# Splitting the last 64 rows of a weight matrix once, apart from the rest

## The chip, the cores and the metric

The kernel runs on one NeuronCore of one Trainium2 chip. The metric is the device time in microseconds (us) of one execution, as the median of several runs. The profile comes from one more execution. TensorE (PE) does the matrix products, VectorE (DVE), ScalarE (ACT) and GpSimd (POOL) the elementwise work, and all transfers are issued from the queue of SyncE (SP).

## The reference

A sequence of 2048 tokens with 576 features goes through a layernorm, linear attention with 32 heads and, beside it, a feed-forward network (FFN) with 4608 hidden features; the FFN's output gates the attention's. Everything is float32.

```python
xn = _layernorm(x)                       # x: [1, 2048, 576]
# attention: q, k, v = xn @ wqkv in 32 heads of 18 features
phi = lambda t: jnp.where(t > 0, t + 1, jnp.exp(t)) + 1e-6
kv = jnp.einsum("bhsd,bhse->bhde", phi(k), v);  z = phi(k) summed over s
s = ((phi(q) @ kv) / (phi(q) @ z + 1e-6)) @ wo
# FFN: w1 [576, 4608], w2 [4608, 576]
g = silu(gelu(xn @ w1 + b1) @ w2 + b2)
out = x + s * g
```

## The kernel before

**Number format.** PE multiplies in a reduced format, fp32r. To keep float32 accuracy each operand is split into a high part (an ACT copy to fp32r, "hi") and a low part (the rest, by a DVE subtraction, "lo"), and a product is the sum of three matmuls: hi x hi, hi x lo and lo x hi.

**Phase 1 (0 to about 155 us)** loops over 16 tiles of 128 tokens, `t` = 0 to 15, one per 9.05 us. In each turn PE projects keys and values (`project`, L222), transposes a later tile (`transpose_x`, L199) and adds up the attention's state (`state`, L259). `layernorm(t + 2)` runs on DVE, POOL (`mv`, L176) and ACT (`xn`, L194). Since nothing else needs it yet, the loop also makes differences of blocks of `w2` for the FFN: `w2_sum` (POOL, L291), `w2_hi` (ACT, L299), `w2_lo` (DVE, L304), `w2_store` (L309), with raw loads `w2_load` (L277). `zacc` (POOL, L425) sums the keys.

**Phase 2 (to about 291 us)** makes queries and the attention's output `s`.

**Phase 3, the FFN**, works on halves of 1024 tokens with 9 chunks of 512 hidden features each: 18 steps. Both matrix products of a step use a 2x2 block scheme with 7 products in place of 8 (Strassen's, in Winograd's form), whose operands are sums and differences of blocks. The up-projection of a step handles two *pairs* of `w1`, `n = 2 * step` and `n + 1`; `Up.step` takes the seven products in the order `UP = (1, 6, 7, 5, 2, 3, 4)`, each seven matmuls of 128x512 (L901): three for each of two blocks of 128 rows, and one for the last rows. Those, 64 of `w1`'s 576 and so 32 in each half of the block scheme, are put together as three copies of 32 rows on the partitions of one tile (`r`), two hi and one lo, so that one matmul makes all three products. Results are combined on DVE: `b` (L927), `e` (L934), `zy` (L938), `mid` (L921, L924), with an ACT copy `mid` (L918) and the GELU on ACT (`g`, L909). Then come 14 groups of 12 down matmuls (`product`, L1031), each added into the accumulator `macc` by DVE (L1040).

**The operands of w1.** In the first half, class `W1` loads a pair raw (`w1raw`, 768 KB, L621; the last rows already copied three times by the host, hence `WT = 6` blocks), makes the differences `T` on POOL (L636 to L645), the hi parts on ACT (L649) and the lo parts on DVE: L657 for the whole blocks and L659 for the 32 partitions of the last rows' lo part. The finished tiles are kept in DRAM (`keep_op`, L600). In the second half class `W1Loaded` (L682) loads them back. Tiles `a`, `c` and `d` (10 blocks of 128 columns) hold two operands each, from a ring of four buffers; tile `6` holds one, from two buffers.

**The operands of w2.** `W2.hi` (L603) and `W2.lo` (L606) split the pieces of `w2` that phase 1 has not made. L603 and L606 also split the hidden activations `h`.

**The bias b2.** `start_with_b2` (L867) fills `macc` with copies of `b2` by two broadcast transfers, at step 0 and again at step 9.

**Order.** A step has 28 slots: `base + 7j + k` behind product `k` of pair `j`, then `base + 14 + 2k + q` behind the down groups. `add(slot, fn)` puts work into a slot, and DVE, ACT, POOL and PE execute in exactly that order; the SP queue's order is the scheduler's. Tables place the work: `P1` for the odd pair during its own step, `P0` for the next step's even pair, `PW2` for `w2`.

Of the kernel before, what the change touches and what calls it, by code (L numbers as in the profile page):

```python
# [15 lines left out]
P = 128  # L16
# [8 lines left out]
KT = 5  # L25
WT = 6
NF = F // P
# [12 lines left out]
@with_exitstack  # L40
def linear_attention_gated_ffn(ctx, tc, x, wqkv, wo, w1, b1, w2, b2, out):
    nc = tc.nc
# [68 lines left out]


    rr_dram = dram.tile([2, P, 512], F32, name="rr_dram")
    rq_dram = dram.tile([2, 8, P, 512], F32, name="rq_dram")
    c_dram = dram.tile([2, P, QH, 2, HD], F32, name="c_dram")

# [194 lines left out]

    W2_LOADS = {0: (0, 1), 1: (2,), 3: (3,), 4: (4,), 5: (5,), 8: (6,), 9: (7,), 12: (8,)}
    W2_SUMS = {}
# [80 lines left out]
    for t in range(NT):  # L394
        if t + 3 < NT:
            load_x(t + 3)
        pk = bank2(f"pk{t}")
        project(t, wk_h, wk_l, pk)
        if t == 0:
            for k in range(KT):  # L400
                split_w(raw_v[k], k, wv_h, wv_l, nc.vector)
        if t + 1 < NT:
            if t + 1 in (8, 12):
                x_block((t + 1) // 4)
            transpose_x(t + 1)
        for j in W2_SUMS.get(t - 1, ()):
            w2_hi(j)
        for j in W2_SUMS.get(t - 1, ()):
            w2_lo(j)
        if t + 2 < NT:  # L410
            layernorm(t + 2)
        k_t, _ = phi(t1, pk, f"k{t}")
        if pend is not None:
            state(*pend)
        pv = bank2(f"pv{t}")
        project(t, wv_h, wv_l, pv)
        v_t = t1.tile([P, D], F32, tag="v", name=f"v{t}")
        nc.scalar.copy(as2(v_t), pv[:, :, :HD])
        if t + 2 < NT:
            normalize_x(t + 2)  # L420
        if t == 0:
            nc.gpsimd.memset(zacc, 0.0)
        for j in W2_SUMS.get(t, ()):
            w2_sum(j)
        nc.gpsimd.tensor_tensor(zacc, zacc, k_t, op=ADD)  # L425
        for k in WQ_SPLITS.get(t, ()):
            split_w(raw_q[k], k, wq_h, wq_l, nc.gpsimd if k == 0 else nc.vector)
        for k in WQ_LOADS.get(t, ()):
            raw_q[k] = load_w_raw(0, k)
        for j in W2_SUMS.get(t - 1, ()):  # L430
            w2_store(j)
        for c in W2_LOADS.get(t, ()):
            w2_load(c)
        if t == KT + 2:
            make_mask()
            nc.gpsimd.memset(kvz, 0.0)
        pend = (t, k_t, v_t)
        if t in (4, 8):
            b = t // 4 - 1
            if b == 0:  # L440
                nc.sync.dma_start(x_dram[:, 0:4], xh[0][:, :4].bitcast(F32))
                nc.sync.dma_start(x_dram[:, 4:8], xl[0].bitcast(F32))
            else:
                nc.sync.dma_start(x_dram[:, 10:12], xh[1][:, 2:4].bitcast(F32))
                nc.sync.dma_start(x_dram[:, 14:16], xl[1][:, 2:].bitcast(F32))
# [162 lines left out]


    def w1_tile(i, n):  # L610
        k, tag, bufs = (5, "w6", 2) if i == 6 else (10, "wa", 4)
        return w1p.tile([P, k, P], F32R, tag=tag, name=f"w{i}_{n}", bufs=bufs)

    class W1:


# [11 lines left out]
        def T(self, i):  # L628


            a, b = slice(0, 3), slice(3, 6)
            f0, f1, src = self.f0, self.f1, self.src
            tt = EW1.tensor_tensor
            if i == 5:
                src[5] = f0[:, a]
                tt(src[5], f1[:, a], f0[:, a], op=SUB)  # L636
            elif i == 6:
                src[6] = w1p.tile([P, 3, P], F32, tag="w1t6", name="w1t6", bufs=1)
                tt(src[6], f1[:, b], src[5], op=SUB)
            elif i == 7:  # L640
                src[7] = f1[:, a]
                tt(src[7], f1[:, b], f1[:, a], op=SUB)
            else:
                src[4] = f0[:, b]
                tt(src[4], f0[:, b], src[6], op=SUB)  # L645

        def hi(self, i):
            self.tiles[i] = t = w1_tile(i, self.n)
            nc.scalar.copy(t[:, : 3 if i == 6 else 6], self.src[i])  # L649

        def lo(self, i):
            t, src = self.tiles[i], self.src[i]
            n = 1 if i == 6 else 2
            by3 = lambda v: v.rearrange("p (h k) c -> p h k c", h=n)
            hi, src = by3(t[:, : 3 * n]), by3(src)
            lo = t[:, 3 * n :].rearrange("p (h k) c -> p h k c", h=n)
            EL1.tensor_tensor(lo, src[:, :, :2], hi[:, :, :2].bitcast(F32), op=SUB)  # L657
            r = hi[64:96, :, 2]
            EL1.tensor_tensor(r, src[64:96, :, 2], r.bitcast(F32), op=SUB)  # L659
            keep_op(w1_dram, (self.n, i), t)  # L660

        def product(self, i):

            if i == 6:
                t = self.tiles[6]
                return t[:, :2], t[:, 3:], t[:, 2]
            key, k = {1: "a0", 2: "a1", 7: "c0", 3: "c1", 5: "d0", 4: "d1"}[i]
            t, k = self.tiles[key], int(k)
            return t[:, 3 * k : 3 * k + 2], t[:, 6 + 2 * k : 8 + 2 * k], t[:, 3 * k + 2]

    class W1Loaded(W1):


        def __init__(self, n):
            self.n, self.tiles = n, {}
            for i in ("a", 6, "c", "d"):
                if i == "c":
                    t = w1r.tile([P, 10, P], F32R, tag="stw", name=f"wc_{n}")
                else:
                    t = w1_tile(i, n)  # L680
                self.tiles[i] = t
                nc.sync.dma_start(t.bitcast(F32), w1_dram[n % NP, i])  # L682
# [17 lines left out]
    class Rest:  # L700
# [30 lines left out]
        def split(self, k):  # L731
# [3 lines left out]
            nc.vector.tensor_tensor(l, src, h.bitcast(F32), op=SUB)  # L735
            for n, v in enumerate((h, l, h, h)):
                nc.sync.dma_start(
                    rq_dram[self.half, 4 * k : 4 * k + 4, 32 * n : 32 * n + 32], v.bitcast(F32)
                )
# [8 lines left out]

    def load_rest(half, i, dst):
        nc.sync.dma_start(dst.bitcast(F32), rq_dram[half, REST_AT[i]])  # L750

# [24 lines left out]
    def beside(i, k):  # L776
# [15 lines left out]
        else:  # L792
# [16 lines left out]
            if i == 13:  # L809
                w1t[1] = W1(1)  # L810
            if i == 16:
                z = xsum[1]
                load_rest(1, 1, z.h0[:, 4])
                load_rest(1, 6, z.tiles[0][:, 4])
                load_rest(1, 7, z.h1[:, 4])
            if i == 17:
# [4 lines left out]
                w.hi(6), w.lo(6)  # L821
            if i == 18:
                w = w1t[0]
                for j in ("c", "d"):
# [39 lines left out]
    C11, C12, C21, C22, U1 = range(5)  # L864
    def start_with_b2():
        for b in range(2):
            nc.sync.dma_start(  # L867
                macc[:, :, 2 * b : 2 * b + 2].rearrange("p q h d -> p q (h d)"),
                bass.AP(tensor=b2.tensor, offset=b2.offset, ap=[[0, P], [0, QH], [1, D]]),
            )  # L870

# [149 lines left out]
    def product(c, i, q2, hs, w, held):  # L1021
# [14 lines left out]
        src, dst = ps[:, :, :HD], macc[:, q2 : q2 + 2, DST[i], :]  # L1036
        if c == 0 and i == 1:
            nc.vector.tensor_copy(dst, src)
        else:
            nc.vector.tensor_tensor(dst, src, dst, op=ADD)  # L1040

# [9 lines left out]
    def load_xs(t):  # L1051
        F = lambda v: v.bitcast(F32)
        if t in (0, 3):
            raw = stage_w1(f"xs{t}")
            xt, s_t = raw[:, :D], raw[:, KT * P : KT * P + D]
        elif t < 5:
            raw = w1_tile("a", f"xs{t}") if t < 4 else fr.tile(
                [P, 2, D], F32R, tag="w2_5", name="xs4", bufs=1
            )
            raw = F(raw).rearrange("p a b -> p (a b)")  # L1060
            xt, s_t = raw[:, :D], raw[:, D : 2 * D]
        else:
# [132 lines left out]
    def plan_w1(add, w, base, T, hi, lo):  # L1195
# [5 lines left out]
        T={5: 1, 6: 1, 7: 1, 4: 2},  # L1201
        hi={"a": 0, 6: 2, "c": 4, "d": 5},
        lo={"a": 0, 6: 3, "c": 4, "d": 6},
    )
# [39 lines left out]
    xs = x_operands(z.h0, z.l0, z.h1, z.l1, s1, s2, s4, load_rests(1, (5, 2, 3, 4)))  # L1244
    add(0, start_with_b2)
    seq = ExitStack()
    seq.enter_context(in_order(nc.vector.engine, nc.scalar.engine, nc.gpsimd.engine, nc.tensor.engine))
    n_chunks = 2 * NC
    for step in range(n_chunks):
# [4 lines left out]
        if half == 0:  # L1254
            plan_w1(add, w1t[2 * step + 1], base, **P1)
            add(base + 2, w2t[step].sum7)
            for i, at in PW2.items():
                add(base + at, w2t[step].hi, i)
                add(base + at, w2t[step].lo, i)
            if step == 0:  # L1260
                for i, at in W2_SUMS_FIRST.items():
                    add(at, w2t[0].load, i)
        if half == 0 and c < NC - 1:
            add(base + 0, make, W1, w1t, 2 * step + 2)
# [33 lines left out]
        if half == 1 and c == 0:  # L1298
# [4 lines left out]
            add(base + 1, silu_first, C22)  # L1303
            add(base + 7, start_with_b2)
        if half == 1 and 1 <= c <= 8:
# [7 lines left out]
        if plain:  # L1313
            for m in (C12, C21, C22):
                add(base + 4, combine, m, nc.gpsimd)
            for t, at in enumerate((5, 5, 7, 13, 5, 12, 12, 12)):
                add(base + at, load_xs, t)
# [68 lines left out]
```

## Time and profile before

| what | value |
|---|---|
| time, median of 3 runs | 1178.38 us (1176.27 to 1181.19) |
| profiled execution | 1179.5 us |
| its span | 1177.7 us |
| mean granted TensorE clock | 0.979 |
| busy PE, DVE, ACT, POOL | 1123.4, 852.0, 465.7, 461.7 us |
| moved by DMA | 269.36 MB, mean 229 GB/s |

The span runs from the first to the last recorded instruction of that execution. "Busy" is the time in which the engine executes, without issuing transfers and waiting. In the lists of instructions a line gives start, duration, engine, source line, operation, `output<-inputs` with shapes and, in square brackets, the idle time just before with what ended it.

### The profile page before, as it was taken

What the parts mean: (1) busy time and instruction counts of PE and PEld (TensorE: products, weight loads), DVE (VectorE), ACT (ScalarE), POOL (GpSimd) and SP (SyncE); (2) the same over time, 40 slices, a digit from 0 to 9 for tenths busy, and PEclk for the clock granted to TensorE, in tenths of its full rate; (3) what the DMA queues carried; (4) which work ended last, traced back from release to release, by engine and by line L of the source; (5) the groups of instructions that cost most, each with busy time, mean ns of one, the idle gap of its engine ahead of it and who ended that gap; (6) DMA issues with size and microseconds to landing.
All of it is one profiled execution on the core that took longest, in us unless ns stands there. A gap on an engine that the chain in (4) does not pass through costs nothing.

```text
span 1177.7 us, 18497 instructions
## 1 busy us (share of the span) xinstructions
PE 1123.4 (95%) x6972; PEld 1028.9 (87%) x6972; DVE 852.0 (72%) x1226; ACT 465.7 (40%) x766; POOL 461.7 (39%) x372
## 2 busy tenths in 40 slices
PE   8999999999698989889898999979999999999998
PEld 8999989999497978879797887969989989989987
DVE  6666649898487888888888888754855855756756
ACT  4444443334344444443434444432332332332433
POOL 4555624333244452534545244231341341332340
PEclk9999999999899999999999999999999999999999
DMA  7577632665967647484663849997767676676452
GB/s 281 201 294 285 237 101 77 199 233 197 305 261 264 225 167 299 154 320 151 249 252 140 309 177 347 411 319 268 255 221 216 220 228 216 219 223 221 135 168 106
DMA packets 80472, 269.36 MB, mean 229 GB/s; under 512 B 8829, under 2 KB 19325, under 8 KB 76799
## 3 DMA queue, kind: packets, MB, share of 16 engines
q1 hardware_dynamic: 80383, 268.18, 65.4%
q8 instruction: 55, 0.90, 0.3%
q14 instruction: 34, 0.28, 0.1%
HBM read 166.27 MB, written 99.94 MB: 226 GB/s over the span
## 4 chain that ended last, share of the span: by engine, by line
PE 79%; DVE 10%; issue 5%; DMA 3%; ACT 2%; POOL 0%; DVEq 0%; ACTq 0%; POOLq 0%
PE pm L1031 30%; PE e L901 8%; PE zy L901 7%; PE a L901 6%; PE pk L222 5%; PE pv L222 5%; PE ps_s L579 5%; PE pq L222 4%; PE b L901 4%; PE pd L1143 2%; DMA op<-w__3588 1%; PE ps_kva L259 1%; DVE h_l L606 1%; DMA kr<-kw 1%; DVE macc L1040 1%
## 5 line engine op out<-in xcount | busy, mean ns | idle before, releaser
L1040 DVE TENSOR_TENSOR macc<-pm,macc 128x576 f32<-128x576 f32 x234 | 176.5, 754 | 70.2 <-PE pm L1031 62.7
L603 ACT CAST h_h<-g 128x512 fp32r<-128x512 f32 x204 | 120.8, 620 | 147.0 <-PE pm L1031 145.9
L606 DVE TENSOR_TENSOR h_l<-g,h_h 128x512 fp32r<-128x512 f32 x204 | 157.4, 779 | 0.0
L1000 POOL TENSOR_TENSOR mid<-g 128x512 f32<-128x512 f32 x34 | 44.9, 1320 | 151.2 <-ACT g L909 151.2
L994 POOL TENSOR_TENSOR g<-g 128x512 f32<-128x512 f32 x34 | 54.6, 1606 | 67.0 <-DVE h_l L606 65.7
L636 POOL TENSOR_TENSOR w1raw<-w1raw 128x384 f32<-128x384 f32 x18 | 21.9, 1216 | 126.3 <-issue 126.3
L918 ACT COPY mid<-a 128x512 f32<-128x512 f32 x36 | 21.1, 587 | 116.5 <-PE a L901 116.5
L901 PE MATMUL a<-xh,wa 128*128 128x512 f32 x162 | 56.5, 403 | 10.1 <-ACT mid L918 10.1
L909 ACT ACTIVATE g<-b,b1c 128x512 f32<-128x512 f32 x36 | 24.8, 689 | 103.9 <-DVE b L927 103.9
L921 DVE TENSOR_TENSOR mid<-b,mid 128x512 f32<-128x512 f32 x36 | 24.9, 691 | 44.3 <-PE b L901 40.7
L1118 POOL TENSOR_TENSOR fin1l<-fin1h,fin1l 128x288 f32<-128x288 f32 x8 | 6.5, 809 | 127.7 <-DMA fin1l<-s_dram 84.0
L997 POOL TENSOR_TENSOR g<-g 128x512 f32<-128x512 f32 x34 | 54.9, 1613 | 2.7
L901 PE MATMUL a<-h0r,wa 128*128 128x512 f32 x162 | 54.7, 391 | 0.0
L901 PE MATMUL e<-s,wc 128*128 128x512 f32 x108 | 34.8, 467 | 19.2 <-DVE b L927 19.2
L909 ACT ACTIVATE g<-e,b1c 128x512 f32<-128x512 f32 x36 | 24.8, 688 | 59.0 <-DVE e L934 59.0
L901 PEld LDWEIGHTS a<-xh,wa 128*128 128x128 f32 x162 | 30.9, 191 | 19.4 <-ACT mid L918 13.0
L991 POOL TENSOR_TENSOR g<-g 128x512 f32<-128x512 f32 x34 | 46.3, 1361 | 2.7
L901 PEld LDWEIGHTS e<-s,wc 128*128 128x128 f32 x108 | 22.9, 219 | 27.8 <-DVE b L927 22.9
L544 POOL TENSOR_TENSOR pbuf<-phiq,den 128x576 f32<-128x576 f32 x16 | 20.0, 1251 | 65.8 <-DVE den L543 48.8
L606 DVE TENSOR_TENSOR h_l<-mid,h_h 128x512 fp32r<-128x512 f32 x34 | 44.0, 1295 | 1.2
L934 DVE TENSOR_TENSOR e<-e,mid 128x512 f32<-128x512 f32 x36 | 25.0, 693 | 23.7 <-PE e L901 23.6
L291 POOL TENSOR_TENSOR w2r<-w2r 128x576 f32<-128x576 f32 x27 | 41.8, 1553 | 0.7
(799 smaller groups left out, 3659.0 us busy)
## 6 DMA issues: line engine op xcount, KB each, us to landing
op<-w2o SPq DMA_DIRECT2D x27, 576.0 KB
w1raw<-w SPq DMA_DIRECT2D x18, 768.0 KB
w2raw<-w SPq DMA_DIRECT2D x10, 1152.0 KB
op_a<-wa SPq DMA_DIRECT2D x18, 640.0 KB
op_c<-wc SPq DMA_DIRECT2D x18, 640.0 KB
op_d<-wd SPq DMA_DIRECT2D x18, 640.0 KB
wc<-op_c SPq DMA_DIRECT2D x18, 640.0 KB
wa<-op_a SPq DMA_DIRECT2D x18, 640.0 KB
```

Of the source, the lines that this page charges most:

```text
L222: nc.tensor.matmul(ps[:, h, :HD], st, w[:, k, h * HD : (h + 1) * HD], start=(i == 0), stop=(i == len(seq) - 1),)
L579: nc.tensor.matmul(ps[:, h, :HD], st[:, k, :], w[:, k, h * HD : (h + 1) * HD], start=(i == 0), stop=(i == len(seq) - 1),)
L603: nc.scalar.copy(pair[0], src)
L606: eng.tensor_tensor(pair[1], src, pair[0].bitcast(F32), op=SUB)
L901: nc.tensor.matmul(ps, st, mv, start=first and n == 0, stop=n == len(seq) - 1, skip_group_check=True,)
L909: nc.scalar.activation(g, ps, AF.Gelu_apprx_tanh, bias=b1c[:, f : f + 1])
L991: tt(src[5, pr], A(1, 0), A(1, 1), op=ADD)
L994: tt(src[6, pr], src[5, pr], A(0, 0), op=SUB)
L997: tt(src[3, pr], A(0, 1), src[6, pr], op=SUB)
L1000: tt(src[7, pr], A(0, 0), A(1, 0), op=SUB)
L1031: nc.tensor.matmul(ps[:, q, :HD], hs[p][st][:, cs], m[:, p, :], start=(n == 0 and i not in CHAIN), stop=(n == len(seq) - 1), skip_group_ch ...
L1040: nc.vector.tensor_tensor(dst, src, dst, op=ADD)
```

## The change

The last 64 rows of `w1` leave the tiles of the pairs. A new input `w1e` (5 x 128 x 512, laid out by the host) holds them for four pairs at a time on 128 partitions (32 rows each). Phase 1 loads the five pieces (`we_load`, t = 1 to 4, 256 KB each), makes the four differences on POOL (`we_sums`, t = 1 to 5), the hi and lo parts of seven operands at once on ACT and DVE (`we_hi`, `we_lo`, 128x896, t = 2 to 6), and stores them (`we_store`, two transfers of 448 KB). In phase 3 one transfer a pair, `load_we` (448 KB), brings them back into a tile of seven blocks, with two buffers. The tiles of `w1` shrink (`WT = 4`; raw 512 KB, `a`, `c`, `d` 8 blocks, `6` 4 blocks), L659 is gone, `a`, `c` and `d` get a ring of five buffers and `6` one buffer. In the second half the `6` operands of two pairs of a step share one such tile, `e`. On the side of the tokens the last rows' four copies become hi, hi, lo, lo in place of hi, lo, hi, hi. The bias comes from a tile `b2b`, loaded once, that DVE adds in the first chunk's products 2, 3, 4 and 7; `start_with_b2` is gone. In the plans the hi parts of `c` and `d` and the lo part of `d` of the odd pair come one slot earlier, and the lo parts of `w2` one slot later. The raw load of `w2`'s chunk 5 moves from t = 5 to t = 6, and the final tiles' inputs (`load_xs`) go to other slots and buffers. PE's instructions stay the same in number and shape.

```diff
 KT = 5
-WT = 6
+WT = 4
+WG = 5
+WB = 7
 NF = F // P
...
         nc.sync.dma_start(d, w2op.pop(j).bitcast(F32))
-    W2_LOADS = {0: (0, 1), 1: (2,), 3: (3,), 4: (4,), 5: (5,), 8: (6,), 9: (7,), 12: (8,)}
+    we = {}
+    def we_load(q):
+        if not we:
+            we["u"] = x_lo(2, "w1u").rearrange("p a b -> p (a b)").bitcast(F32)
+            we["h", 0] = x_lo(3, "w1h0").rearrange("p a b -> p (a b)")
+            we["h", 1] = x_hi(3, "w1h1").rearrange("p a b -> p (a b)")
+        u = we["u"][:, (q % 2) * 1024 : (q % 2) * 1024 + 1024]
+        we[q] = u.rearrange("p (b c) -> p b c", b=8)
+        nc.sync.dma_start(u[:, :512], w1e[q])
+    def we_sums(q):
+        u = we[q]
+        for dst, a, b in ((4, 0, 1), (5, 3, 0), (6, 3, 4), (7, 2, 6)):
+            nc.gpsimd.tensor_tensor(u[:, dst], u[:, a], u[:, b], op=SUB)
+    def we_op(q, v):
+        return we["h", q % 2][:, v * WB * P : (v + 1) * WB * P]
+    def we_hi(q):
+        nc.scalar.copy(we_op(q, 0).rearrange("p (b c) -> p b c", b=WB), we[q][:, 1:])
+    def we_lo(q):
+        h, l = (we_op(q, v).rearrange("p (b c) -> p b c", b=WB) for v in range(2))
+        nc.vector.tensor_tensor(l, we[q][:, 1:], h.bitcast(F32), op=SUB)
+    def we_store(q):
+        d = we_dram.rearrange("(g q) v r c -> q v g r c", q=WG)
+        for v in range(2):
+            nc.sync.dma_start(d[q, v], we_op(q, v).bitcast(F32))
+    W2_LOADS = {0: (0, 1), 1: (2,), 3: (3,), 4: (4,), 6: (5,), 8: (6,), 9: (7,), 12: (8,)}
     W2_SUMS = {}
...
             load_x(t + 3)
+        if t == 1:
+            we_load(0), we_load(1)
         pk = bank2(f"pk{t}")
...
             w2_lo(j)
+        if 2 <= t < 2 + WG:
+            we_hi(t - 2), we_lo(t - 2)
         if t + 2 < NT:
...
             w2_sum(j)
+        if 1 <= t < 1 + WG:
+            we_sums(t - 1)
         nc.gpsimd.tensor_tensor(zacc, zacc, k_t, op=ADD)
...
             w2_store(j)
+        if 2 <= t < 2 + WG:
+            we_store(t - 2)
+            if t < WG:
+                we_load(t)
         for c in W2_LOADS.get(t, ()):
...
     def w1_tile(i, n):
-        k, tag, bufs = (5, "w6", 2) if i == 6 else (10, "wa", 4)
+        k, tag, bufs = (4, "w6", 1) if i == 6 else (8, "wa", 5)
         return w1p.tile([P, k, P], F32R, tag=tag, name=f"w{i}_{n}", bufs=bufs)
+    we_sb = {}
+    def load_we(n):
+        we_sb[n] = w1p.tile([P, WB, P], F32R, tag="we", name=f"we_{n}", bufs=2)
+        src = we_dram[n % NP]
+        nc.sync.dma_start(
+            we_sb[n].bitcast(F32).rearrange("p b c -> p (b c)"),
+            bass.AP(tensor=src.tensor, offset=src.offset, ap=[[0, 2], [WB * P, 64], [1, WB * P]]),
+        )
+    WE_AT = {1: 0, 2: 1, 3: 2, 5: 3, 7: 4, 6: 5, 4: 6}
     class W1:
...
         def T(self, i):
-            a, b = slice(0, 3), slice(3, 6)
+            a, b = slice(0, 2), slice(2, 4)
             f0, f1, src = self.f0, self.f1, self.src
...
             elif i == 6:
-                src[6] = w1p.tile([P, 3, P], F32, tag="w1t6", name="w1t6", bufs=1)
+                src[6] = w1p.tile([P, 2, P], F32, tag="w1t6", name="w1t6", bufs=1)
                 tt(src[6], f1[:, b], src[5], op=SUB)
             elif i == 7:
-                src[7] = f1[:, a]
-                tt(src[7], f1[:, b], f1[:, a], op=SUB)
+                tt(f1[:, a], f1[:, b], f1[:, a], op=SUB)
             else:
-                src[4] = f0[:, b]
-                tt(src[4], f0[:, b], src[6], op=SUB)
+                tt(f0[:, b], f0[:, b], src[6], op=SUB)
         def hi(self, i):
             self.tiles[i] = t = w1_tile(i, self.n)
-            nc.scalar.copy(t[:, : 3 if i == 6 else 6], self.src[i])
+            nc.scalar.copy(t[:, : 2 if i == 6 else 4], self.src[i])
         def lo(self, i):
             t, src = self.tiles[i], self.src[i]
-            n = 1 if i == 6 else 2
-            by3 = lambda v: v.rearrange("p (h k) c -> p h k c", h=n)
-            hi, src = by3(t[:, : 3 * n]), by3(src)
-            lo = t[:, 3 * n :].rearrange("p (h k) c -> p h k c", h=n)
-            EL1.tensor_tensor(lo, src[:, :, :2], hi[:, :, :2].bitcast(F32), op=SUB)
-            r = hi[64:96, :, 2]
-            EL1.tensor_tensor(r, src[64:96, :, 2], r.bitcast(F32), op=SUB)
+            k = 2 if i == 6 else 4
+            EL1.tensor_tensor(t[:, k:], src, t[:, :k].bitcast(F32), op=SUB)
             keep_op(w1_dram, (self.n, i), t)
         def product(self, i):
+            r = we_sb[self.n][:, WE_AT[i]]
             if i == 6:
                 t = self.tiles[6]
-                return t[:, :2], t[:, 3:], t[:, 2]
+                return t[:, :2], t[:, 2:], r
             key, k = {1: "a0", 2: "a1", 7: "c0", 3: "c1", 5: "d0", 4: "d1"}[i]
-            t, k = self.tiles[key], int(k)
-            return t[:, 3 * k : 3 * k + 2], t[:, 6 + 2 * k : 8 + 2 * k], t[:, 3 * k + 2]
+            t, k = self.tiles[key], 2 * int(k)
+            return t[:, k : k + 2], t[:, 4 + k : 6 + k], r
     class W1Loaded(W1):
...
             self.n, self.tiles = n, {}
-            for i in ("a", 6, "c", "d"):
+            for i in ("a", "c", "d"):
+                if n % 2 and i == "a":
+                    t = w1_tile("e", n)
+                    for k in range(2):
+                        six = t[:, 4 * k : 4 * k + 4]
+                        nc.sync.dma_start(six.bitcast(F32), w1_dram[(n - 1 + k) % NP, 6])
+                        (w1t[n - 1] if k == 0 else self).tiles[6] = six
                 if i == "c":
-                    t = w1r.tile([P, 10, P], F32R, tag="stw", name=f"wc_{n}")
+                    t = w1r.tile([P, 8, P], F32R, tag="stw", name=f"wc_{n}")
                 else:
...
             nc.vector.tensor_tensor(l, src, h.bitcast(F32), op=SUB)
-            for n, v in enumerate((h, l, h, h)):
+            for n, v in enumerate((h, h, l, l)):
                 nc.sync.dma_start(
...
             if i == 16:
+                load_we(0)
                 z = xsum[1]
...
             if i == 18:
+                load_we(1)
                 w = w1t[0]
...
     C11, C12, C21, C22, U1 = range(5)
-    def start_with_b2():
-        for b in range(2):
-            nc.sync.dma_start(
-                macc[:, :, 2 * b : 2 * b + 2].rearrange("p q h d -> p q (h d)"),
-                bass.AP(tensor=b2.tensor, offset=b2.offset, ap=[[0, P], [0, QH], [1, D]]),
-            )
+    b2b = fl.tile([P, D], F32, name="b2b")
+    nc.sync.dma_start(b2b, bass.AP(tensor=b2.tensor, offset=b2.offset, ap=[[0, P], [1, D]]))
+    BIAS = {2: 0, 7: 1, 3: 1, 4: 0}
     def load_rests(half, some):
...
         src, dst = ps[:, :, :HD], macc[:, q2 : q2 + 2, DST[i], :]
-        if c == 0 and i == 1:
+        if c > 0 or i in (5, 6):
+            nc.vector.tensor_tensor(dst, src, dst, op=ADD)
+        elif i in BIAS:
+            h = BIAS[i]
+            bb = b2b[:, None, h * HD : (h + 1) * HD].to_broadcast([P, 2, HD])
+            nc.vector.tensor_tensor(dst, src, bb, op=ADD)
+        else:
             nc.vector.tensor_copy(dst, src)
-        else:
-            nc.vector.tensor_tensor(dst, src, dst, op=ADD)
     def combine(s, eng, q=slice(0, QH)):
...
         T={5: 1, 6: 1, 7: 1, 4: 2},
-        hi={"a": 0, 6: 2, "c": 4, "d": 5},
-        lo={"a": 0, 6: 3, "c": 4, "d": 6},
+        hi={"a": 0, 6: 2, "c": 3, "d": 4},
+        lo={"a": 0, 6: 3, "c": 4, "d": 5},
     )
...
                 add(base + at, w2t[step].hi, i)
-                add(base + at, w2t[step].lo, i)
+                add(base + at + 1, w2t[step].lo, i)
             if step == 0:
...
                     add(at, w2t[0].load, i)
+        if not plain:
+            add(base + 7, load_we, 2 * step + 2)
+            add(base + 14, load_we, 2 * step + 3)
         if half == 0 and c < NC - 1:
...
             add(base + 1, silu_first, C22)
-            add(base + 7, start_with_b2)
         if half == 1 and 1 <= c <= 8:
...
                 add(base + 4, combine, m, nc.gpsimd)
-            for t, at in enumerate((5, 5, 7, 13, 5, 12, 12, 12)):
+            for t, at in enumerate((6, 7, 12, 13, 5, 12, 12, 12)):
                 add(base + at, load_xs, t)
...
     x = np.ascontiguousarray(np.asarray(A_x, f32).reshape(S, D))
-    def w1_tiles(w):
-        w = np.asarray(w, f32)
-        z = np.zeros((32, w.shape[1]), f32)
-        parts = []
-        for h in range(2):
-            r = w[512 + 32 * h : 544 + 32 * h]
-            parts += [w[256 * h : 256 * h + 256], r, r, r, z]
-        return np.concatenate(parts, axis=0).reshape(WT, P, w.shape[1])
+    def w1_last(w):
+        r = np.zeros((2, 32, 4 * WG, 2, P), f32)
+        r[:, :, :NP] = np.asarray(w, f32)[512:].reshape(2, 32, NP, 2, P)
+        blocks = np.stack([r[0, :, :, 1], r[0, :, :, 0], r[1, :, :, 0], r[1, :, :, 1]])
+        blocks = blocks.reshape(4, 32, 4, WG, P).transpose(3, 2, 1, 0, 4)
+        return np.ascontiguousarray(blocks).reshape(WG, P, 4 * P)
     def k_tiles(w):
...
     wqkv = np.ascontiguousarray(k_tiles(A_wqkv))
-    w1 = np.ascontiguousarray(w1_tiles(B_w1).reshape(WT, P, NP, 2, P).transpose(2, 1, 3, 0, 4)).reshape(NP, P, 2 * WT * P)
+    w1 = np.asarray(B_w1, f32)[:512].reshape(WT, P, NP, 2, P).transpose(2, 1, 3, 0, 4)
+    w1 = np.ascontiguousarray(w1).reshape(NP, P, 2 * WT * P)
     wo = np.ascontiguousarray(np.asarray(A_wo, f32))
...
     arrays = {
-        "x": x, "wqkv": wqkv, "wo": wo, "w1": w1, "b1": b1,
+        "x": x, "wqkv": wqkv, "wo": wo, "w1": w1, "w1e": w1_last(B_w1), "b1": b1,
         "w2": np.ascontiguousarray(
```

More of the change, by code (lines that the diff above doesn't have):

```diff
@@ L40, in linear_attention_gated_ffn @@
 @with_exitstack
-def linear_attention_gated_ffn(ctx, tc, x, wqkv, wo, w1, b1, w2, b2, out):
+def linear_attention_gated_ffn(ctx, tc, x, wqkv, wo, w1, w1e, b1, w2, b2, out):
     nc = tc.nc
@@ L114, in linear_attention_gated_ffn @@
     rq_dram = dram.tile([2, 8, P, 512], F32, name="rq_dram")
+    we_dram = dram.tile([4 * WG, 2, 32, WB * P], F32, name="we_dram")
     c_dram = dram.tile([2, P, QH, 2, HD], F32, name="c_dram")
@@ L1052, in load_xs @@
         F = lambda v: v.bitcast(F32)
[L1053 to L1061, printed above, removed]
+        flat = lambda v: F(v).rearrange("p a b -> p (a b)")[:, :D]
+        if t == 0:
+            xt, s_t = flat(w1_tile("a", "x0")), stage_w1("s0")[:, :D]
+        elif t == 1:
+            xt = flat(w1_tile("a", "x1"))
+            s_t = flat(w1p.tile([P, WB, P], F32R, tag="we", name="s1", bufs=2))
+        elif t == 2:
+            xt, s_t = (flat(w1_tile("a", f"{v}2")) for v in "xs")
+        elif t == 3:
+            xt, s_t = stage_w1("x3")[:, :D], flat(w1_tile("a", "s3"))
+        elif t == 4:
+            raw = F(fr.tile([P, 2, D], F32R, tag="w2_5", name="xs4", bufs=1))
+            xt, s_t = raw[:, 0], raw[:, 1]
         else:
@@ L1244, in linear_attention_gated_ffn @@
     xs = x_operands(z.h0, z.l0, z.h1, z.l1, s1, s2, s4, load_rests(1, (5, 2, 3, 4)))
-    add(0, start_with_b2)
     seq = ExitStack()
```

## The prediction

> **What bounds the kernel now.** I read the page first, then TensorE's waits, then windows cut at the step starts (the first of a step's seven matmuls into `a`, from the chain of waits), then timelines of single steps. The page says that PE is busy nearly all the time:
>
> ```profile
> PE 1123.4 (95%) x6972; PEld 1028.9 (87%) x6972; DVE 852.0 (72%) x1226; ACT 465.7 (40%) x766; POOL 461.7 (39%) x372
> PE 79%; DVE 10%; issue 5%; DMA 3%; ACT 2%; POOL 0%; DVEq 0%; ACTq 0%; POOLq 0%
> ```
>
> The change leaves every matmul, so only PE's waits, and the clock lost behind them, can be won. The waits of PE (total us, times, longest):
>
> ```profile
> PE e L901 <- DVE b L927: 19.5, 8, 3.0
> PE a L901 <- ACT mid L918: 10.1, 1, 10.1
> PE e L901 <- DVE wd L657: 5.9, 9, 1.0
> PE pm L1031 <- issue: 5.7, 1, 5.7
> PE pm L1031 <- DVE macc L1040: 3.0, 9, 1.5
> ```
>
> Eight or nine times each, so once a step of the first half; and two large single ones. Windows of step 0, a step of the first half, step 9 and a step of the second half (columns: window, its us, busy us of PE, PEld, DVE, ACT, POOL, granted clock, DMA share, GB/s):
>
> ```profile
> 291.50:351.20 59.70, 48.39 (x269) 42.61 (x268) 39.19 (x57) 24.00 (x39) 22.50 (x17) 0.89 0.83 290
> 452.90:504.10 51.20, 47.37 (x267) 41.71 (x266) 42.25 (x59) 21.94 (x36) 22.87 (x17) 0.97 0.61 226
> 754.30:808.50 54.20, 46.98 (x267) 42.37 (x266) 30.95 (x41) 19.06 (x28) 14.48 (x10) 0.94 0.97 326
> 898.50:943.50 45.00, 45.00 (x267) 40.81 (x266) 28.27 (x39) 14.56 (x24) 14.60 (x12) 1.00 0.68 221
> ```
>
> The same 267 matmuls fill 45.0 us at full clock: that is the floor of a step. Step 0 takes 59.7, steps 1 to 7 take 50.9 (starts 351.15 to 707.61), step 8 46.64, step 9 54.2, steps 10 to 16 45.0. Above the floor lie 14.7 + 7 x 5.92 + 1.64 + 9.2 = 67.0 us, the most that the FFN can give.
>
> **Steps 1 to 8.** The 5.92 is 3.05 (`b`) + 0.62 (`wd`) + 0.20 (`macc`) and about 2.05 of reduced clock behind the 3.05. In the step from 452.9, PE has the work ahead of `e` done at 473.16 and starts it at 476.21. It waits for `b` L927, which is late by DVE's own queue:
>
> ```profile
> 460.53 0.99 DVE L659 TENSOR_TENSOR w<-w1t,w 32x128 fp32r<-32x128 f32 x1
> 464.08 0.42 DVE L659 TENSOR_TENSOR wc<-w1raw,wc 32x256 fp32r<-32x256 f32 x1
> 467.94 0.76 DVE L606 TENSOR_TENSOR w__5070<-w2raw,w__5070 128x576 fp32r<-128x576 f32 x1 [2.05 <-ACT w__5070 L603]
> 469.93 0.42 DVE L659 TENSOR_TENSOR wd<-w1raw,wd 32x256 fp32r<-32x256 f32 x1
> 472.06 1.42 DVE L659 TENSOR_TENSOR wa<-w1raw,wa 32x256 fp32r<-32x256 f32 x1
> 475.46 0.70 DVE L927 TENSOR_TENSOR b<-e,mid 128x512 f32<-128x512 f32 x1
> ```
>
> The change takes the four L659 out of this queue (0.99 + 0.42 + 0.42 + 1.42 = 3.25 us); the other splits keep their shapes, a one-line low part over four blocks being the 128x512 of today. So `b` starts at 475.46 - 3.25 = 472.2. PE needs it earlier than today, as 0.62 and 0.20 ahead are gone too: 473.16 - 0.82 = 472.3, and from the start of `b` to that of `e` there are 0.75, so 471.6. That alone would leave 0.6 us. But the 2.05 in which DVE sat idle for ACT's `w2` high part close in part: the `w2` low parts are one slot later, behind `wd`. Walking the queue with the row durations gives `b` at 470.4 to 471.1, 0.5 to 1.2 us to spare. Low part `wd` moves up a slot, hence the 0.62 goes; the `w2` low part leaves its place in front of `macc`, hence the 0.20. ACT gets its `c` and `d` casts a slot sooner and two thirds as wide (128x768 takes 0.83, 128x512 0.62). POOL's sums narrow from 128x384 (1.02) to 128x256 (about 0.76, from the line through 1.02 and the 1.41 of 128x576). What is late next is `w1`'s raw load: its splits begin at about 468.5 in this step, the load goes out at 457.47 and lands by about 464.5 today, and shrinks from 768 to 512 KB. Gain 7 x 5.92 + 1.64 = 43.1; if the 2.05 do not close, 0.6 x 8 = 4.8 of it stay. I leave 2 as lost, for the whole FFN.
>
> **Step 0.** The wait of 10.1 stands on the chain as one piece:
>
> ```profile
> 303.61 15.61 DMA op<-w__3588
> 319.26 0.04 ACT wa L649
> ```
>
> The name is that of a neighbouring store; what ACT's cast wants is `w1raw`, issued at 299.67 behind the two 1152 KB broadcasts `macc<-b` (issued 296.45). While these land the DMAs are full (share 0.99) at 164 GB/s in 304 to 312; elsewhere a full share gives 415 (314 to 326). The change removes both broadcasts for one of 288 KB, issued before. What then lies ahead of `w1raw` is about 2.6 MB and its own 0.5, landing near 302 to 307 at 290 to 415 GB/s; the cast has place for it until 307. The wait, 0.97 + 0.20 and the clock (PEclk 0.50 in 314 to 326, about 3.4) go: 14.7. Of this up to 3 stay at the slow bound, inside the 2 or in the range.
>
> **Step 9.** The same two broadcasts at 771.42 make the DMA run at 168 GB/s in 780 to 788; `macc` L1040 waits for them, PE 1.47 and 5.75 (shown as issue), with 2 of clock: 9.2, gone. The bias now comes in as second operand of an add that DVE makes anyway (`macc<-pm,macc`, 0.754 mean), so it costs nothing.
>
> **Moved DMAs.** Per pair 448 KB of last rows come in, 256 KB less raw and 448 KB less stores go: a first-half step carries 10.7 MB in place of 11.2. In 45 us that is 238 GB/s, against 226 to 326 in the windows. `load_we` waits on SP for a buffer that the product one slot ahead frees (1.6 us a slot at most, with stores and the next raw load queued behind it; nobody needs these within 20 us). In the second half the two `6` operands of two pairs travel in one tile, the same 4480 KB a step. No gain or loss there: PE is at 45.00 of 45.00, DMA share 0.68.
>
> **Phase 1 pays.** For t = 2 to 6, DVE gets one subtraction of 128x896 (by 0.68 for 128x512 and 0.76 for 128x576: 1.07 to 1.16) between the `w2` low parts and the layernorm of the token tile two ahead, and POOL gets four 128x128 sums (about 0.5 each by the line above; 2.0) before the `zacc` add. The layernorm chain has little room:
>
> ```profile
> 55.50 3.10 POOL L291 TENSOR_TENSOR w2r<-w2r 128x576 f32<-128x576 f32 x2
> 55.57 1.37 DVE L183 SCALAR_TENSOR_TENSOR mv<-mv 128x1 f32<-128x1 f32 x1 [0.73 <-POOL mv L176]
> 56.98 1.20 ACT L194 ACTIVATE xn<-x,mv 128x576 f32<-128x576 f32 x2 [1.01 <-DVE mv L183]
> 58.57 1.40 POOL L425 TENSOR_TENSOR zacc<-zacc,phik 128x576 f32<-128x576 f32 x1
> ```
>
> `xn` is ready at 58.18, the transpose starts at 58.80: 0.62 to spare. The tiny L183 takes 1.37 here, as POOL holds the operands' port; with POOL idle it takes 0.16 (at 20.67). Pushed by 2.0, `zacc` ends at 61.97, and DVE's `w2` low parts, today from 61.30 on, wait 0.67. Cost per token tile 1.07 + 0.67 - 0.62 = 1.12, times five 5.6 us. Bounds: with no collision 0.45 x 5 = 2.3; with the whole add in the way 5 x 1.95 = 9.8; and if each such stall halved the clock, 2.05 more each, 20. ACT's 128x896 cast lies in its waits of a period (1.36 + 1.01 + 2.44), the 896 KB of stores a tile in a phase whose mean DMA share is 0.69.
>
> The Trainium skill (SBUF — State Buffer, "Who interferes with whom") states that a DVE operation with two SBUF inputs and a GpSimd operation that reads SBUF hold a shared port pair exclusively, the loser blocked for the whole instruction. That speaks against this change; 1.37 against 0.16 agrees, and without it the cost would be 2.3. On the clock the skill (TensorE: Matmul & The Clock Gate, "HAM oscillation — how this bites in real kernels") has gaps above some 3.4 us throttle. The trace disagrees: the gap of 3.05 did it (0.72 in 474 to 480), that of 1.47 did not (1.00 in 786 to 790). By the page the end of 20 is out; by the rows it is unlikely.
>
> **Sum.** 1179.5 (profiled time; span 1177.7; the median is 1178.4) - 67.0 + 5.6 + 2 = 1120.
>
> **Rivals.**
> *Half the steps' gain stays away:* the `b` chain is held by something that I walked through by hand, such as POOL's `sum7` or the raw load landing after 468.5, and each step keeps about half of its 5.9. 1120 + 21 = 1141. For it: DVE idles for ACT 2.05 in this very stretch. Against: everything ACT and POOL do there gets shorter.
> *Phase 1 throttles:* 20 in place of 5.6: 1134.
> *One buffer for `w6` (slower):* pair 1's `6` cast on ACT (459.27) now needs pair 0's `6` store, issued at 451.17, to have landed; ACT works in order, so copies to `mid` and activations queue behind it, and PE behind them. In step 0 a transfer took 19.6 us (issued 299.67, cast 319.26). If that store took as long, ACT would stand until 470.8, 11 us in each of nine steps: 1120 + 98 = 1218. It loses from 6.6 us a step (59 / 9). Against: by 451 the 2.3 MB issued from 444 on have about gone at 279 to 453 GB/s, and the 256 KB then need a few us of the 8 there are.
> *Nothing gained:* the waits move to the next late thing one for one: 1179.
>
> **Chances.** Forecast 0.60, half gain 0.18, phase 1 0.09, `w6` 0.08, nothing 0.05. Range 1112 (phase 1 at 2.3, nothing left over, and 2 below) to 1144 (over half gain and throttling): 0.84 less some tails. A change of 0.5% (5.9 us) is about what a measurement of this kernel can tell from no change: faster 0.87, same 0.04, slower 0.09.
>
> **What would show it.** Right: steps 0 to 8 start 45 us apart, `PE e <- DVE b` and the 10.1 and 5.7 gone, phase 1 some 5 us longer with waits of `pt` for `xn`. Wrong: `ACT w <- DMA` waits of several us in steps 1 to 8 (`w6`), `b` still late, a clock below 0.9 before 155 us, or second-half steps above 45.

## The result, and the profile after

The changed kernel takes 1249.6 us (median of 4, 1246.6 to 1251.0) against 1179.8 for the kernel before: ratio 1.059 (95% interval 1.056 to 1.063). The forecast was 1120. The profiled execution took 1251.0, its span is 1249.2. From the page (busy time of the engines; the chain by engine):

```profile
PE 1136.9 (91%) x6972; PEld 1044.1 (84%) x6972; DVE 816.6 (65%) x1159; ACT 456.7 (37%) x771; POOL 448.4 (36%) x392
PE 59%; DMA 27%; DVE 4%; SPq 3%; POOL 2%; issue 2%; ACT 1%; POOLq 0%; DVEq 0%; ACTq 0%
```

DVE has 35 us less to do, as meant. But DMA holds 27% of the chain where it held 3%. The waits of PE (total, times, longest):

```profile
PE pt L203 <- ACT xn L198: 37.0, 6, 19.3
PE pm L1089 <- ACT h_h L650: 17.6, 6, 5.3
PE b L959 <- issue: 7.7, 1, 7.7
PE a L959 <- DMA xh<-rq_dram: 5.9, 1, 5.9
```

Of what was named in the prediction, the waits for `wd`, for `macc` and the single one of 10.1 are gone, and that for `b` stands there once in place of eight times. Windows of step 0, step 3, step 9 and step 12 (columns as in the prediction):

```profile
336.30:394.90 58.60, 49.70 (x268) 43.62 (x267) 33.97 (x48) 22.39 (x38) 20.06 (x17) 0.91 0.68 239
490.60:535.60 45.00, 45.00 (x268) 40.81 (x267) 36.75 (x50) 20.35 (x36) 20.45 (x17) 1.00 0.66 245
760.60:826.50 65.90, 50.02 (x268) 43.10 (x267) 32.07 (x42) 19.13 (x28) 15.04 (x10) 0.84 0.79 266
934.90:984.00 49.10, 46.78 (x267) 42.26 (x267) 28.60 (x38) 14.78 (x24) 15.16 (x12) 0.97 0.61 190
```

Steps 2 to 8 sit on the floor of 45.0 us, as forecast. The rest does not: the FFN starts at 336.3 in place of 291.5, steps 0 and 1 take 58.6 and 50.7, step 9 takes 65.9, and steps 10 to 16 take 49.2 to 54.4 where they took 45.0. The balance of the two profiled executions, step starts against step starts: 44.8 ahead of the FFN, 19.8 in steps 0 to 16 (86.6 above 45 each, against 66.8 before), 6.9 in the tail; 71.5 in all.

The lines that explain it are two windows in which hardly anything but one of the new transfers runs: the end of the first `load_we` (issued at 328.95) with what stands behind it, and a stretch of `we_store` (PE and everything else idle):

```profile
340.50:344.50 4.00, 0.75 (x2) 0.68 (x3) 0.00 (x0) 0.00 (x0) 0.00 (x0) 0.79 0.13 50
95.00:101.00 6.00, 0.00 (x0) 0.00 (x0) 0.00 (x0) 0.00 (x0) 0.00 (x0) 0.50 0.24 84
```

With work queued, the 16 DMA engines are busy 0.13 and 0.24 of the time, about 2/16 and 4/16, and move 50 and 84 GB/s, against some 400 where a queue of wide transfers runs (395 in e3, 299 to 306 us). An access pattern `ap=[[step, count], ...]` lists its dimensions from the outermost to the innermost, and a step of 0 repeats the same rows. `load_we` reads `ap=[[0, 2], [896, 64], [1, 896]]`, outermost dimension 2; `we_store` writes `d[q, v]` of form `g r c`, outermost dimension 4.

Whatever is issued behind them waits for the few engines that they fill. The trace's completion marks, 16 for a wide transfer, show it: `load_we` ends with marks at 342.70 and 342.96, and of the 16 of `xh<-rq_dram`, issued just behind it at 329.56, fourteen have come by 335.53 and the last two come at 343.36 and 343.62. PE's wait of 5.9 is for that one. In phase 1 this makes 35.8 of the 44.8, as e2 below shows. The chain that leads to a late token tile there is a 256 KB load issued behind narrow stores, a narrow store, and the load of the tile (start, duration, transfer):

```profile
66.78 22.41 DMA w1u<-w1e
89.25 25.18 DMA we_dram<-w1h
115.97 16.49 DMA x<-x
```

In the second half it shows on SP, whose issues normally take 0.3 to 1 us (at most 3.1 in the kernel before). It shows as well on POOL, which waits for the inputs of finished tokens, such as `fin4h`, while the sums `mid` that make the next hidden operands stand behind them in its order. The last two lines are POOL's waits for one such input, in the kernel before and in the changed one:

```profile
913.34 0.51 SPq L666 DMA_DIRECT2D we<-we_dram  x1
915.42 10.12 SPq L1029 DMA_DIRECT2D w__8968<-op  x1
928.85 18.28 DMA fin4h<-x
```

```profile
POOL fin1l L1118 <- DMA fin1l<-s_dram: 84.0, 6, 14.9
POOL fin1l L1184 <- DMA fin1l<-s_dram: 155.6, 5, 33.6
```

### The profile page after: what moved, and what is told of

Same layout as the page of the kernel before. It is cut to its first block, busy times and chain, and to the rows that moved or that the text cites. A ratio compares the mean times of both kernels' runs of the same rounds, so it can differ in the third digit from the quotient of the medians.

```text
span 1249.2 us, 18534 instructions
## 1 busy us (share of the span) xinstructions
PE 1136.9 (91%) x6972; PEld 1044.1 (84%) x6972; DVE 816.6 (65%) x1159; ACT 456.7 (37%) x771; POOL 448.4 (36%) x392
## 4 chain that ended last, share of the span: by engine, by line
PE 59%; DMA 27%; DVE 4%; SPq 3%; POOL 2%; issue 2%; ACT 1%; POOLq 0%; DVEq 0%; ACTq 0%
PE pm L1089 24%; PE e L959 6%; PE zy L959 6%; PE a L959 5%; DMA w1u<-w1e 3%; PE pv L226 3%; PE pq L226 3%; PE b L959 3%; DMA fin4h<-x 3%; PE pk L226 3%; PE ps_s L626 2%; DMA we<-op 2%; DMA we_dram<-w1h 2%; DMA fin2h<-x 2%; PE pd L1209 2%
## 5 line engine op out<-in xcount | busy, mean ns | idle before, releaser
L1096 DVE TENSOR_TENSOR macc<-pm,macc 128x576 f32<-128x576 f32 x218 | 164.4, 754 | 68.1 <-PE pm L1089 66.5
L653 DVE TENSOR_TENSOR h_l<-g,h_h 128x512 fp32r<-128x512 f32 x204 | 168.1, 829 | 6.9 <-ACT h_h L650 6.6
L979 DVE TENSOR_TENSOR mid<-b,mid 128x512 f32<-128x512 f32 x36 | 24.7, 687 | 61.1 <-PE b L959 59.4
L694 POOL TENSOR_TENSOR w1raw<-w1raw 128x256 f32<-128x256 f32 x18 | 16.9, 937 | 130.6 <-DVE wa L710 130.6
L959 PE MATMUL a<-xh,wa 128*128 128x512 f32 x144 | 51.7, 399 | 6.9 <-ACT g L967 3.8
L959 PE MATMUL a<-h0r,wa 128*128 128x512 f32 x144 | 50.6, 392 | 0.0
L982 DVE TENSOR_TENSOR mid<-zy,mid 128x512 f32<-128x512 f32 x36 | 24.9, 691 | 37.3 <-PE zy L959 37.2
L203 PE MATMUL pt<-ident,xn 128*128 128x128 f32 x80 | 13.5, 306 | 38.3 <-ACT xn L198 37.0
L985 DVE TENSOR_TENSOR b<-e,mid 128x512 f32<-128x512 f32 x36 | 25.2, 699 | 31.7 <-PE e L959 31.6
L959 PE MATMUL b<-s2r,we 128*128 128x512 f32 x126 | 34.7, 418 | 12.0 <-issue 7.7
L203 PEld LDWEIGHTS pt<-ident,xn 128*128 128x128 f32 x80 | 10.2, 155 | 40.4 <-ACT xn L198 38.6
```

What stands on the lines that cost most here:

```text
L653: eng.tensor_tensor(pair[1], src, pair[0].bitcast(F32), op=SUB)
L959: nc.tensor.matmul(ps, st, mv, start=first and n == 0, stop=n == len(seq) - 1, skip_group_check=True,)
L985: tt(B, E, u2_sb, op=ADD)
```

## The experiments

Theory N says that narrow transfers are the whole loss; rival Q blames the longer SP queue, rival D the added work and the new rings of buffers. Each run gives its time in us and, in brackets, its ratio to the kernel before with the 95% interval; steps are those of its profiled execution.

**e1.** The load as two transfers of 64 rows.

```diff
-        nc.sync.dma_start(we_sb[n]..., bass.AP(..., ap=[[0, 2], [WB * P, 64], [1, WB * P]]))
+        rows = bass.AP(tensor=src.tensor, offset=src.offset, ap=[[WB * P, 64], [1, WB * P]])
+        for k in range(2):
+            nc.sync.dma_start(dst[64 * k : 64 * k + 64], rows)
```

> Only load_we is changed: two transfers of 64 rows x 3584 B in place of one whose outermost dimension is the 2 copies (zero stride) of 64 rows. Theory N (narrow transfers: a transfer runs on no more of the 16 DMA engines than its outermost dimension has entries, so 2 for load_we and 4 for we_store): the FFN's waits go, steps 1 to 17 start 45 us apart again, about 80 of the 86 us that the steps of the changed kernel have above 45 are won; phase 1 keeps its 45 us more; 1163 to 1172 us. Rival Q (the SP queue: more and larger transfers behind each other, whatever their form): one more issue a pair, so 1245 to 1260. Rival D (phase 1's extra DVE and POOL work and the new buffer rings are at fault): no change, 1249.

Measured: 1155.2 (ratio 0.980, 0.977 to 0.983). Step 0 takes 45.9, every other step 45.0; the FFN still starts at 335.1. The load cost the FFN 86 us and the tail 7 more, where N's range had counted on about 80. Q and D are out for the load.

**e2.** The stores as four parts each.

```diff
-            nc.sync.dma_start(d[q, v], we_op(q, v).bitcast(F32))
+            for g in range(4):
+                nc.sync.dma_start(d[q, v, g], we_op(q, v)[32 * g : 32 * g + 32].bitcast(F32))
```

> Only we_store is changed: each of its two transfers a token tile (outermost dimension 4) becomes four of 32 rows x 3584 B, eight a token tile. Theory N: phase 1 gets back 35 to 40 of the 45 us that it got longer, the FFN keeps its steps of 49 to 66 us; 1205 to 1215 us. Rival Q: eight issues in place of two make the queue longer, 1250 to 1290. Rival D: phase 1 unchanged, 1249.

Measured: 1213.9 (1.030, 1.027 to 1.033), in N's range. The FFN starts at 300.6, its steps are as slow as in the changed kernel (85.6 above 45 each). Q is out for the stores too: four times the issues made it faster.

**e3.** Both edits.

> Both edits at once. Theory N: 1120 to 1135, the forecast's sum with phase 1 some 5 to 10 us longer than before. Rivals Q and D: above 1230.

Measured: 1119.6 (1118.4 to 1120.8; ratio 0.950, 0.947 to 0.952). The gains of e1 and e2, 94.4 and 35.8, add up to that of e3, 130.0. All steps but step 9 (45.6) take 45.0 to 45.1; windows of step 0, step 3 and step 12:

```profile
299.20:344.30 45.10, 45.10 (x269) 40.86 (x268) 35.46 (x48) 22.38 (x38) 20.10 (x17) 1.00 0.90 329
434.30:479.30 45.00, 45.00 (x268) 40.81 (x268) 36.75 (x50) 20.34 (x36) 20.46 (x17) 1.00 0.69 246
839.90:884.90 45.00, 45.00 (x269) 40.81 (x268) 28.26 (x38) 14.56 (x24) 15.14 (x13) 1.00 0.75 220
```

**e4.** The kernel before with the bias tile alone.

```diff
-    add(0, start_with_b2)
...
-            add(base + 7, start_with_b2)
+            bb = b2b[:, None, h * HD : (h + 1) * HD].to_broadcast([P, 2, HD])
+            nc.vector.tensor_tensor(dst, src, bb, op=ADD)
```

> The kernel before with one part of the change alone: the bias comes from the tile b2b (one 288 KB broadcast), the two 1152 KB broadcasts into macc at steps 0 and 9 are gone. The prediction's terms for steps 0 and 9 stand on these broadcasts: 14.7 + 9.2 less, 1156. If step 0's wait for w1raw belongs to the other transfers queued there, only step 9 gains: 1170.

Measured: 1159.2 (0.984, 0.982 to 0.986), 19.4 less. Step 9 takes 45.0 (from 54.2), step 0 takes 50.4 (from 59.5). So the broadcasts are worth 9.2 in step 9 and 9.1 in step 0, where 14.7 was expected; what stays in step 0, 5.4, is the late `b` that every first-half step has (steps 1 to 7: 50.1 to 50.9).

**e5, e6.** From e3, the same two loads with the DRAM side written as (2, 32 rows, 896) and (4, 16 rows, 896).

```diff
-ap=[[WB * P, 64], [1, WB * P]]
+ap=[[32 * WB * P, 2], [WB * P, 32], [1, WB * P]]
```

> From e3. load_we stays two transfers of 64 rows x 3584 B from the same addresses to the same partitions; only the notation of the DRAM side changes, from (64 rows, 896) to (2, 32 rows, 896). Theory N: each transfer falls back to 2 engines (DMA share about 0.13, 50 GB/s while alone), the FFN's steps grow as in e2: 1185 to 1225 us. If the form of the notation doesn't matter and e1's gain came from having two issues, or from the zero stride being gone: 1120.

> As e5, with (4, 16 rows, 896). Theory N: 4 engines, 448 KB at about 100 GB/s take 4.5 us in place of 9: a part of the waits only, 1122 to 1160. Otherwise 1120.

Measured: 1119.5 and 1118.7, as e3. By itself this fits the other reading that was named, so N was not shown yet: two issues, or the zero stride, could have been it. But the transfer that ran was the same: in the traces the instruction carries its destination as [64, 1] rows of 3584 B in e3, e5 and e6 alike. So the rows, which lie without a gap, had been joined to 64 before, and nothing was tested.

**e9, e10.** So the same with a gap: one unused row behind each 32, or each 16, in the DRAM copy.

```diff
-    we_dram = dram.tile([4 * WG, 2, 32, WB * P], F32, name="we_dram")
+    we_dram = dram.tile([4 * WG, 2, 33, WB * P], F32, name="we_dram")
...
+ap=[[33 * WB * P, 2], [WB * P, 32], [1, WB * P]]
```

> From e3. e5 and e6 may have changed nothing because their dimensions lie without gaps and can be joined into one. Here the DRAM copy has one unused row behind each 32, so that the two transfers of load_we, 64 rows x 3584 B each, keep (2, 32 rows, 896) as their form: no zero stride, two issues, same bytes. Theory N: 2 engines a transfer, DMA share about 0.13 at 50 GB/s while alone; the FFN's steps grow as in e2 (sum of steps 0 to 16 about 90 us above 45 each), 1190 to 1220. If e1's gain came from two issues in place of one, or from the zero stride being gone: 1120.

> As e9 with one unused row behind each 16: (4, 16 rows, 896). we_store's parts get the form (2, 16 rows, 896) with it, so phase 1 is disturbed and only the FFN's steps are read. Theory N: 4 engines, so the 448 KB take half of e9's time; steps 0 to 16 in sum 5 to 60 us above 45 each. Otherwise all at 45.

Measured: e9 takes 1217.9 (1.033, 1.029 to 1.037), its instruction now carries [1, 64], its steps are about those of e2 (59.9, 50.9, 45.0 seven times, 65.1, then 45.3 to 59.4; 88.6 above 45 each), and it has the same row where its load runs alone:

```profile
306.00:310.00 4.00, 0.40 (x1) 0.43 (x2) 0.00 (x0) 0.00 (x0) 0.00 (x0) 0.54 0.13 51
```

Two issues, no zero stride, the bytes of e3, and only the outermost dimension at 2: that settles N for the load. With 4 (e10, a single run of 1207.0) step 0 takes 53.0, step 9 takes 53.4 and all others 45.0: 16.4 above 45 each. So 2, 4 and 64 entries cost the FFN some 87, 16 and 1 us. e10 also tests the stores: eight issues of 32 rows in both, but of outermost dimension 2 in e10, and its FFN starts at 369.8 where that of e9 starts at 301.8.

**e7.** From e3, phase 1 in another order.

```diff
-        if 2 <= t < 2 + WG:
-            we_hi(t - 2), we_lo(t - 2)
         if t + 2 < NT:
             layernorm(t + 2)
         k_t, _ = phi(t1, pk, f"k{t}")
+        if 2 <= t < 2 + WG:
+            we_hi(t - 2), we_lo(t - 2)
...
         nc.gpsimd.tensor_tensor(zacc, zacc, k_t, op=ADD)
+        if 1 <= t < 1 + WG:
+            we_sums(t - 1)
```

> From e3. Phase 1 in another order: we_hi and we_lo come behind phi instead of ahead of the layernorm chain, we_sums behind the zacc add. Theory C (the port collision of zacc with the w2 low parts and the 1.08 us of we_lo lie in the layernorm chain, as in the prediction): the waits of pt for xn (6.0 us in e3) go, the FFN starts 5 to 7 us earlier, 1112 to 1115. Rival (phase 1 is longer by its transfers or by the engines' load): 1119, same.

Measured: 1120.7, no gain over e3, so Theory C's range is missed. The five waits of 1.1 to 1.5 are gone, as it said, but one of 6.2 has come, with slow clock behind it (0.78 in 74.5 to 83.5). On the chain of waits it stands as the load of a token tile, issued behind eight stores, a load of 1152 KB and two copies of 1024 KB:

```profile
66.44 11.19 DMA x<-x
```

**e11, e12.** From e7, first one store a token tile (hi and lo part of a row beside each other, 128 outermost), then also the two 1024 KB copies three tiles later.

```diff
-        for v in range(2):
-            for g in range(4):
-                nc.sync.dma_start(d[q, v, g], ...)
+        nc.sync.dma_start(we_dram[q], we["h", q % 2][:, : 2 * WB * P].bitcast(F32))
...
-        if t in (4, 8):
+        if t in (7, 8):
```

> From e7, with one store a token tile in place of eight: the DRAM copy keeps the hi and lo part of a row beside each other (128 rows x 7168 B, all 128 outermost), and the x side's last rows are interleaved to match. e7 lost the 6 us that it had won to one wait for a token tile that was loaded behind the eight stores. Theory C: that wait goes too, the FFN starts at 292 to 294, 1112 to 1115. Rival (phase 1's transfers are simply too many bytes there): the wait stays, 1118 to 1121.

> From e11, with the two 1024 KB copies of the first token tiles (x_dram, at t = 4) issued at t = 7, when the pieces of w1's last rows are through. In e11 the one wait of phase 1 that is left (4.5 us, and slow clock behind it) is for a token tile whose 288 KB took 13.7 us to land behind those copies. If that pile of bytes at one place is what is left of phase 1's price: no wait, the FFN starts at 291 to 293, 1111 to 1114. If the bytes are too many for the whole stretch, the wait moves to another tile: 1117 to 1119.

Measured: e11 1118.0 (0.949, 0.947 to 0.951), the FFN starts at 296.6 and one wait of 4.5 is left, as its rival said: the eight issues were only a part of it. e12 1112.5 (1111.9 to 1113.2; ratio 0.943, 0.941 to 0.945), no wait of `pt` for ACT left, the FFN starts at 290.1, as expected for a pile of bytes at one place. It beats both kernels.

**e8.** From e3, the plan's slots of the kernel before.

```diff
-        hi={"a": 0, 6: 2, "c": 3, "d": 4},
-        lo={"a": 0, 6: 3, "c": 4, "d": 5},
+        hi={"a": 0, 6: 2, "c": 4, "d": 5},
+        lo={"a": 0, 6: 3, "c": 4, "d": 6},
...
-                add(base + at + 1, w2t[step].lo, i)
+                add(base + at, w2t[step].lo, i)
```

> From e3, with the plan's slots as in the kernel before: hi parts of c and d at 4 and 5, lo part of d at 6, w2's lo parts in the slot of their hi parts. The prediction's walk: taking out L659 leaves b some 0.6 us late in steps 1 to 8, the wait for wd (0.62) and for macc (0.20) come back: 1.2 to 1.5 us in each of nine steps, 1130 to 1133. If narrower tiles and the absence of L659 alone are enough: 1120.

Measured: 1132.8 (0.960, 0.958 to 0.963), 13 above e3. The profile is of an execution of 1138.5; the other three took 1131.1 to 1133.0. In it steps 0 to 7 take 46.2, 9.7 more than in e3 together, with `b` late by 0.40 and an operand `h_l` by 0.46; step 8 takes 45.0. Another 8 lie in step 9 (49.5) and ahead of the FFN, which starts 4 us later; the edit changes first-half steps alone, and no run shows whether the other executions have these 8. So the slots are worth about 10 us, a little less than the walk's 10.8 to 13.5 (1.2 to 1.5 in nine steps), and of its parts only the first came: no wait for `wd` or `macc` is back. That the median lies in its range is partly luck.

## Why the prediction was wrong

**The step that failed** is "Moved DMAs" ("No gain or loss there"), and in "Phase 1 pays" the sentence on the 896 KB of stores. Both priced transfers by their bytes (238 GB/s a step; "a phase whose mean DMA share is 0.69") and took none of the new ones' form into account. Terms set at nothing measured 94.4 (e1: 86 in the FFN, 7 in the tail, 1 ahead of the FFN) and 35.8 (e2). The loss of 130 is all of the miss: e3, which only widens the same transfers, comes to 1119.6 where 1120 was forecast. That it comes so near is partly luck: in e3's profile the FFN's steps give back 66.1, one more than the 65.0 that were counted on, and phase 1 costs 7.7, two more than the 5.6.

**It could have been read from the trace before.** That kernel has narrow transfers of its own, the stores `rq_dram[half, 4k : 4k + 4, ...]` in phase 2, outermost dimension 4. A window where they run:

```profile
203.00:206.00 3.00, 3.00 (x25) 3.00 (x24) 2.93 (x4) 0.64 (x1) 0.42 (x1) 1.00 0.25 88
```

A share of 0.25 at 88 GB/s is a row for the width-4 price; by half of that the 448 KB of `load_we` would have been some 10 us each, twice a step, on two engines that all other transfers need too (an estimate). The Trainium skill (DMA: Bandwidth & Descriptors, "Why a DMA increments its semaphore by 16 and not by 1" and "Rules for kernel authors") states the rule: the number of engines is the largest up to 16 that divides the slowest dimension of both access patterns, and "a leading zero-stride broadcast of c copies" confines a transfer to at most c. The runs agree: 0.13 with 2 entries, 0.24 with 4. It says "as the instruction carries it", and e5 and e6 against e9 agree: the forms in their instructions differ, not only those in the program. This was the rule that spoke against the change, and the prediction weighed two others.

**Steps 1 to 8** went as walked: 45.0 once the transfers are wide (e1, e3), and in the changed kernel from step 2 on. In these steps `b` is no longer late, DVE waits for PE there:

```profile
553.45 0.70 DVE L985 TENSOR_TENSOR b<-e,mid 128x512 f32<-128x512 f32 x1 [0.90 <-PE e L959]
```

**Step 0 and step 9**: 9.2 was right for step 9. Of step 0's 14.7 the broadcasts held 9.1 and the `b` chain 5.4 (e4), which the wait of 10.1 had hidden and the term does not name; the sum was right, by luck, as the change removes both.

**Phase 1**: in e3 the FFN starts 7.7 later than before, forecast 5.6. In four turns the period is 10.37 (50.07 to 60.45 is one) in place of 9.05, so 1.32 more, where 1.12 was forecast. A fifth, 1.68 longer, waits for a token tile that is loaded behind the last stores. PE's wait of 1.12 in the line below equals the forecast by chance, as two parts of the sum were off: the `w2` low parts lose 1.16 to POOL's `zacc` add (2.59 for two, from 1.43), not 0.67, and the room was about 0.95, not 0.62, as PE starts 0.92 behind ACT's start and so needs only the first of its two operations on `xn` (0.87, with 0.42 for the second). 1.08 + 1.16 - 0.95 is 1.29. The first line is of the kernel before, the others are of e3:

```profile
52.25 1.43 DVE L304 TENSOR_TENSOR w2o<-w2r,w2o 128x576 fp32r<-128x576 f32 x2
```

```profile
52.51 1.43 POOL L469 TENSOR_TENSOR zacc<-zacc,phik 128x576 f32<-128x576 f32 x1
52.63 2.59 DVE L308 TENSOR_TENSOR w2o<-w2r,w2o 128x576 fp32r<-128x576 f32 x2
55.14 1.08 DVE L341 TENSOR_TENSOR w1h<-w1u,w1h 128x896 fp32r<-128x896 f32 x1
59.53 1.20 ACT L198 ACTIVATE xn<-x,mv 128x576 f32<-128x576 f32 x2 [3.20 <-DVE mv L187]
60.45 0.76 PE L203 MATMUL pt<-ident,xn 128*128 128x128 f32 x5 [1.12 <-ACT xn L198]
```

None of these waits lowered the clock (granted 1.00 throughout e3). e12 shows that the price is not bound to the change: with another order and other transfers its FFN starts at 290.1, ahead of the 291.5 before.

**Signs and rivals.** Three of the signs for being wrong came: second-half steps above 45, a clock below 0.9 ahead of 155 us (0.50 in 95 to 101), and a wait of ACT's cast of `6` for the store of the other pair's, the mechanism of the single `w6` buffer. This last one shows once at length, 9.6 us in step 1:

```profile
ACT w L705 <- DMA op<-w: 12.5, 2, 9.6
```

All three go with the narrow transfers: in e3 the clock stays at 1.00, the second-half steps take 45.0 (step 9 45.6), and this wait is not there. So no rival had named the cause.

**What stays open**: why narrow loads leave steps 2 to 8 at 45.0 and not steps 10 to 16. That in the first half nothing small stands behind them with a near due time, while in the second the inputs of finished tokens do, is read from the queues, and no run isolated it. Open as well is what makes e8's profiled execution 8 us longer outside the steps that its edit changes.

## What to carry to other kernels

Price a new transfer by its form as well as its bytes: look at the outermost dimension of both sides, and look in the trace for a transfer of that form and the DMA share while it runs alone. A narrow transfer costs twice, by its own length and by what queues behind it on the engines that it fills. And a change that loses may hold a winner: here the form of two access patterns stands between 1249.6 and 1119.6 us.

## What the runs showed of the hardware

A transfer whose outermost dimension has 2 entries ran at 50 GB/s (changed kernel, e9), one with 4 at 84 to 88 (changed kernel, kernel before), while a queue of wide ones reached 395 (e3). Of a wide transfer issued behind one with 2 entries, 14 of the 16 marks came by 335.53 and the last two at 343.36 and 343.62 (changed kernel). Dimensions written apart but lying without a gap changed nothing (e5, e6), with a gap of one row they did (e9: 98 us more). While narrow transfers were in flight, one single issue on SP took 10.12 us in place of 0.3 to 1. Two DVE subtractions took 2.59 in place of 1.43 where POOL's `zacc` add ran beside them (e3).
